# Moving the first token shift and the first weights' low parts to TensorE products with diagonal matrices

## The chip, the core and the metric

The program runs on one core of a Trainium2 chip. The metric is the device time of that core in microseconds. A core has TensorE (matmul, PE in the profile), VectorE (DVE), ScalarE (ACT), GpSimd (POOL) and SyncE (SP, which here only issues DMAs).

## The reference, cut to what matters

Three layers follow one another. Inputs are float32 but for the three weights of the second layer, which come as float64.

```python
# 1: attention in chunks of 64, B=8, H=8, S=576, D=64
scores = scale * q_c @ k_c.T ; attn = softmax(scores) ; x = attn @ v_c
# 2: token shift and channel mix, d_model 512, d_ff 1024
xk = mu_k * x + (1 - mu_k) * x_prev ; xr = mu_r * x + (1 - mu_r) * x_prev
k = relu(xk @ w_k) ; v = (k * k) @ w_v ; x = sigmoid(xr @ w_r) * v
# 3: causal attention of 4 experts, the best two of each token weighted by a gate
```

x_prev is x one token earlier in the same sequence, and zero for the first token.

## The kernel before

All products of layers 2 and 3 are made in three reduced-precision (float32r) products: every operand is kept as a high part `hi` (the value rounded to float32r) and a low part `lo = value - hi`, and `mm3` (L53) adds hi·hi, hi·lo and lo·hi.

Layers 1 and 2 are in `attn_mix` (L62). Tokens are cut into 36 tiles of 128 and 12 units of 384. Attention runs on pairs of tiles j: `s_T` (L132) transposes q and k of a tile on TensorE, `s_S` (L144) makes the scores of a pair and its softmax, with five VectorE steps and an exponential on ScalarE, `s_PT` (L138) transposes the probabilities, and `s_PV` (L173) multiplies by v and copies the result into `XT`, a unit's x with channels on partitions. `s_prev` (L211) puts the token before a unit into column 0 of `XT`. The list `attn` (L337) holds these steps in program order: pair 2 is transposed (tiles 4 and 5), then the probabilities of tiles 2 and 3 are turned, and one step `s_SPV` makes the scores of pair 2 and then the v products of pair 1, which complete unit 0.

`s_shift` (L222) makes the shifted input of a unit for w = 1 (xr) and w = 0 (xk), in four groups of 128 channels: ScalarE scales x_prev by 1 - mu, VectorE multiplies x by mu and adds (L240), ScalarE rounds the sum to `hi` (L243), VectorE subtracts for `lo` (L244). `mix_r`, `mix_k` and `mix_v` (L251, L259, L278) are the matmuls of a unit: 48, 96 and 96 products of 128 x 384. Their PSUM tiles are the three buffers with the tag "mix".

The float64 weights are brought to float32 in 20 conversions of 128 x 512 (four of w_r, eight of w_k, eight of w_v): `conv` (L296) loads the raw words over the SP queue into a staging tile `st`, which has two buffers after the first four, and works on ScalarE (L310), GpSimd (L311) and VectorE (L312 to L314); `split` (L322) rounds to `hi` on GpSimd (L46) and subtracts for `lo` on VectorE (L324).

The string `pro` orders the prologue: c is one conversion, a is one step of `attn`, q and v are loads, s is the shift of unit 0. After it, the items of each unit are issued in order, and attention steps are put between them at `rate0` a matmul item for the first two units, and conversions two an item in `mix_r` and one after. This program order is only a priority: the build orders every engine's stream on a simulated time line, and on the chip each engine then takes its stream in that order.

Layer 3 (`experts`, L449) begins behind the last unit and is not touched.

Of the kernel before, what the change touches and what calls it, by code (L numbers as in the profile page):

```python
# [8 lines left out]
F32 = mybir.dt.float32  # L9
F32R = mybir.dt.float32r  # L10
I32 = mybir.dt.int32
ACTF = mybir.ActivationFunctionType
ALU = mybir.AluOpType
# [6 lines left out]

CH = 64
UNIT = 384
CFG = dict(ps=(2, 3, 1, 2), P=5, sm=3, load=6, lag=(3, 4), out=(5, 1), qk1=(1, 1), qk0=(10, 1.2), v=(11, 1), order=(3, 4, 0, 1, 2), after=1, conv='v', clo='v', chi='g', x2hi='g', x2lo='v', ylo='g', yhi='v', xt='aa', r2='av', klo='vg', amul='vg', nearly=2, x2b=1, yb=4, qb=4, direct=((0, 1), (1, 1), (1, 1)), tailAV=4, kp=1, yt=1, yf=2, zb=1, om=(4, 3, 2, 1, 0), hp=1000, x2d=2, early=(2, 1), dact=3, rate0=0.43, rate=0.45, sh=(10, 12, 2), sh2=(11, 1, -1), pro='cccqqaacavvcaaaaacaacaaaascc', alag=2, seq=0, end=2, outL=(10, 2), outE=2, kcp='aa', dsc='v', ldb=2, vb=2, cn=512, stb=2, xb=4, pa=5, tb=2, first_j=7)
SEG = 192


# [7 lines left out]
def eng(nc, c):  # L34
    return nc.vector if c == "v" else nc.gpsimd


def nth(s, i):
    return s[i % len(s)]


def copy(nc, c, out, in_):
    if c == "a":
        nc.scalar.activation(out=out, in_=in_, func=ACTF.Copy)
    else:
        eng(nc, c).tensor_copy(out, in_)  # L46


def f32(ap):
    return ap.bitcast(F32)  # L50


def mm3(nc, out, terms, first=True, last=True):  # L53

    n = len(terms)
    for i, ((ah, al), (bh, bl)) in enumerate(terms):
        nc.tensor.matmul(out=out, lhsT=ah, rhs=bh, start=first and i == 0, stop=False)  # L57
        nc.tensor.matmul(out=out, lhsT=ah, rhs=bl, start=False, stop=False)  # L58
        nc.tensor.matmul(out=out, lhsT=al, rhs=bh, start=False, stop=last and i == n - 1)  # L59


def attn_mix(tc, at, x2T, q, k, v, mu_k, mu_r, w_k, w_v, w_r, ident, attended_all, mixed_k):  # L62

    nc = tc.nc
# [3 lines left out]
    KD = DM // 128  # L68
    FF = w_k.shape[1]
    KF = FF // 128  # L70
    NU = B * S // UNIT
    TPU = UNIT // 128
    NSEG = UNIT // SEG
    CPS = SEG // CH
    scale = 1.0 / float(D) ** 0.5

    with ExitStack() as ctx:
        wts = ctx.enter_context(tc.tile_pool(name="wts", bufs=1))
        mx = ctx.enter_context(tc.tile_pool(name="mx", bufs=1))
        ps = ctx.enter_context(tc.tile_pool(name="psM", bufs=1, space=PSUM))  # L80

        pa_open = ExitStack()
        pa = pa_open.enter_context(tc.tile_pool(name="psA", bufs=1, space=PSUM, side="right"))
        wkr_open = ExitStack()
        wkr = wkr_open.enter_context(tc.tile_pool(name="wkr", bufs=1, side="right"))
# [4 lines left out]
        mu = wkr.tile([128, 2, KD], F32, name="mu")  # L90
        mu1 = wkr.tile([128, 2, KD], F32, name="mu1")
# [3 lines left out]
        def runs(t):  # L95
            b, s = divmod(t * 128, S)
            return [(0, b, s, 128)] if s + 128 <= S else [(0, b, s, CH), (CH, b + 1, 0, CH)]

        def load_qk(t):
            for src, nm in ((q, "q"), (k, "k")):  # L100
                x = at.tile([128, H * D], F32, tag="ld" + nm, bufs=CFG["ldb"], name="ld" + nm)
                for p, b, s, n in runs(t):
                    nc.sync.dma_start(out=x[p:p + n].rearrange("p (h d) -> p h d", h=H),
                                      in_=src[b, :, s:s + n, :].rearrange("h p d -> p h d"))
                qkv[nm, t] = x

        def load_v(t):
            x = at.tile([128, 2, HP, D], F32, tag="ldv", bufs=CFG["vb"], name="ldv")
            for c in range(2):
                b, s = divmod(t * 128 + c * CH, S)  # L110
                for e in range(2):
                    r = e ^ c
                    nc.sync.dma_start(out=x[r * 64:(r + 1) * 64, c],
                                      in_=v[b, e::2, s:s + CH, :].rearrange("g p d -> p g d"))
            qkv["v", t] = x

        qT, kT, PP, PT, XT = {}, {}, {}, {}, {}
        nT = NU * TPU

        def bank(nm):  # L120
            return pa.tile([128, HP, 128], F32, tag="A", bufs=CFG["pa"], name=nm)

        def to_sbuf(src, nm):

            p = bank("Tps")
            for g in range(HP):
                nc.tensor.transpose(p[:, g], src[:, g * 128:(g + 1) * 128], ident)  # L127
            o = at.tile([128, HP, 128], F32, tag=nm, bufs=CFG["tb"], name=nm)
            nc.scalar.activation(out=o, in_=p, func=ACTF.Copy)
            return o  # L130

        def s_T(t):  # L132
            qT[t] = to_sbuf(qkv.pop(("q", t)), "qT")
            kT[t] = to_sbuf(qkv.pop(("k", t)), "kT")
            if t + CFG["ldb"] < nT:
                load_qk(t + CFG["ldb"])

# [67 lines left out]
        def s_SPV(j):  # L205
            if 2 * j < nT:
                s_S(j)
            if j:
                s_PV(j - 1)

        def s_prev(u):  # L211
# [6 lines left out]
                    nc.gpsimd.tensor_copy(x[:, :, sg, 0:1], src[:, :, SEG:SEG + 1])  # L218

        XS = {}  # L220

        def s_shift(u, ws, g):  # L222
            x = XT[u]
            now, prev = x[:, g, :, 1:], x[:, g, :, :SEG]
            by_act = u < CFG["dact"]
            if not by_act:
                d = wkr.tile([128, NSEG, SEG], F32, tag="xa", bufs=2, name="xa")
                nc.gpsimd.tensor_tensor(d, now, prev, op=ALU.subtract)  # L228
            for w in ws:
                nm = "kr"[w]  # L230
                if g == 0:
                    XS[u, w] = Split(wkr.tile([128, KD, UNIT], F32R, tag="xh" + nm, name="xh" + nm),
                                     wkr.tile([128, KD, UNIT], F32R, tag="xl" + nm, name="xl" + nm))
                o = XS[u, w]
                a = d if not by_act and w == ws[-1] else wkr.tile([128, NSEG, SEG], F32, tag="xa" if by_act else "r2", bufs=2, name="xb")
                af = a.rearrange("p s t -> p (s t)")
                m = mu[:, w, g:g + 1]
                if by_act:
                    nc.scalar.activation(out=a, in_=prev, func=ACTF.Copy, scale=mu1[:, w, g:g + 1])
                    nc.vector.scalar_tensor_tensor(a, now, m, a, op0=ALU.mult, op1=ALU.add)  # L240
                else:
                    nc.vector.scalar_tensor_tensor(a, d, m, prev, op0=ALU.mult, op1=ALU.add)  # L242
                nc.scalar.activation(out=o.hi[:, g], in_=af, func=ACTF.Copy)  # L243
                nc.vector.tensor_tensor(o.lo[:, g], af, f32(o.hi[:, g]), op=ALU.subtract)  # L244
# [3 lines left out]
        def rhs(o, g):  # L248
            return o.hi[:, g], o.lo[:, g]

        def mix_r(u, m):  # L251
# [3 lines left out]
            cc = slice(m * 128, (m + 1) * 128)  # L255
            mm3(nc, p, [((wr.hi[:, g, cc], wr.lo[:, g, cc]), rhs(XS[u, 1], g)) for g in range(KD)])
            nc.scalar.activation(out=sig[u][:, m], in_=p, func=ACTF.Sigmoid)  # L257

        def mix_k(u, m):  # L259
            p = ps.tile([128, UNIT], F32, tag="mix", bufs=3, name="mps")  # L260
            cc = slice(m * 128, (m + 1) * 128)
            mm3(nc, p, [((wk.hi[:, g, cc], wk.lo[:, g, cc]), rhs(XS[u, 0], g)) for g in range(KD)])
            r = mx.tile([128, UNIT], F32, tag="r", bufs=2, name="r")
# [30 lines left out]
        done = [0]  # L294
# [26 lines left out]

        def split(z, dst, g, c0, n):  # L322
            copy(nc, CFG["chi"], dst.hi[:, g, c0:c0 + n], z)
            eng(nc, nth(CFG["clo"], done[0])).tensor_tensor(dst.lo[:, g, c0:c0 + n], z, f32(dst.hi[:, g, c0:c0 + n]), op=ALU.subtract)  # L324

        def chunks(src, dst):
# [10 lines left out]
        attn = []  # L337
        for j in range(nT // 2 + 1):
            two = (2 * j, 2 * j + 1)
            attn += [(t // TPU, s_T, t) for t in two if t < nT]  # L340
            attn += [((t - 2) // TPU, s_PT, t - 2) for t in two if t > 1]
            attn.append(((2 * j - 1) // TPU if j else 0, s_SPV, j))
            attn += [(t // TPU, s_prev, t // TPU) for t in (2 * j - 2, 2 * j - 1) if t > 0 and t % TPU == TPU - 1]
        attn.reverse()

        def attend(u, n=1):
# [22 lines left out]
        loads = {"q": iter(range(CFG["ldb"])), "v": iter(range(CFG["vb"]))}  # L369

        def first_shift():
            for ws in ((1, 0),) if CFG["sh2"][2] >= 0 else ((1,), (0,)):
                for g in range(KD):
                    s_shift(0, ws, g)

        for c in CFG["pro"]:
            if c == "a":
                attend(2)
            elif c == "c":
                convert(1)  # L380
            elif c in loads:
                (load_qk if c == "q" else load_v)(next(loads[c]))
            else:
                attended(0)
                first_shift()

        credit = 0.0
        for u in range(NU):
# [6 lines left out]
            for i, (f, *args) in enumerate(items):  # L395
# [10 lines left out]
                if u + 1 < NU:  # L406
                    both = u + 1 <= CFG["sh2"][2]
                    for ws, at0 in (((1, 0), CFG["sh2"][0]),) if both else (((1,), CFG["sh"][0]), ((0,), CFG["sh"][1])):
                        g, r = divmod(i - at0, CFG["sh2" if both else "sh"][1 if both else 2])
# [478 lines left out]
```

## Time and profile before

| | |
|---|---|
| Median of 3 runs | 1052.54 us (1049.31 to 1054.02) |
| Profiled execution | 1051.87 us, span 1050.1 us |
| PE busy | 992.5 us of the span |
| DVE, ACT, POOL busy | 721.4, 583.4, 414.7 us |
| mean granted TensorE clock | 0.990 |

Busy time of TensorE is from the start of an instruction to its modelled end. It overlaps for pipelined instructions, so the pace is read from the distance of starts. Times in rows are microseconds from the start of the span unless they are marked ns.

### The profile page before, as it was taken

How to read it: one execution, taken by the hardware profiler on the slowest of the kernel's cores; microseconds unless marked ns; L12 is line 12 of the kernel's file. 1: busy time of each engine (PE TensorE's matmuls, PEld its weight loads, DVE VectorE, ACT ScalarE, POOL GpSimd, SP SyncE). 2: the span in 40 equal slices, each digit the busy share in tenths (PEclk: the TensorE clock that was granted, in tenths of full speed). 3: DMA queues.
4: the chain of work that ended last, by engine and by line, in shares of the span. 5: the costliest groups of instructions: out<-in, count | busy, mean ns of one | idle time of the engine just before them, and what ended most of it. 6: DMA issues, size and time to landing. Idle time of an engine off the chain costs nothing.

```text
span 1050.1 us, 22252 instructions
## 1 busy us (share of the span) xinstructions
PE 992.5 (95%) x8422; PEld 951.1 (91%) x8422; DVE 721.4 (69%) x1793; ACT 583.4 (56%) x1379; POOL 414.7 (39%) x507
## 2 busy tenths in 40 slices
PE   3679899999999999999999999999999999999997
PEld 2569899998999999999998999999999898998985
DVE  5899745628654856665667622787878687878896
ACT  3479473545354445545353422576776667766674
POOL 5444403526443744454545536423333332313201
PEclk9889999999999999999999999999999999999999
DMA  9774512242323243323213025645361635334212
GB/s 227 201 196 133 128 33 81 49 114 62 101 61 100 49 115 82 81 72 75 65 44 86 16 61 134 133 115 147 73 180 48 189 63 161 102 98 139 71 54 72
DMA packets 167522, 105.27 MB, mean 100 GB/s; under 512 B 133512, under 2 KB 145912, under 8 KB 167416
## 3 DMA queue, kind: packets, MB, share of 16 engines
q1 hardware_dynamic: 132024, 54.55, 20.3%
q0 software_dynamic: 35392, 49.30, 18.0%
q8 instruction: 67, 1.10, 0.4%
q14 instruction: 39, 0.32, 0.1%
HBM read 66.01 MB, written 28.38 MB: 90 GB/s over the span
## 4 chain that ended last, share of the span: by engine, by line
PE 64%; DVE 18%; DMA 6%; ACT 6%; issue 3%; POOL 2%; SPq 0%; ACTq 0%; DVEq 0%; POOLq 0%
PE mps L57 12%; PE mps L59 12%; PE mps L58 12%; PE pj L57 5%; PE pj L58 4%; PE pj L59 4%; PE Tps L663 3%; PE Tps L127 3%; PE AVps L687 2%; DMA out_dram<-o 2%; PE AVps L683 2%; DVE r L271 2%; DVE sm L605 2%; PE Sps L603 1%; PE Sps L602 1%
## 5 line engine op out<-in xcount | busy, mean ns | idle before, releaser
L57 PE MATMUL mps<-xhk,wkh 128*128 128x384 f32 x384 | 131.6, 343 | 0.2
L57 PE MATMUL mps<-kh,wvh 128*128 128x384 f32 x384 | 130.4, 343 | 1.2 <-DVE x2o L288 0.8
L58 PE MATMUL mps<-kl,wvh 128*128 128x384 f32 x384 | 128.9, 337 | 2.5 <-POOL kl L273 2.4
L58 PE MATMUL mps<-xlk,wkh 128*128 128x384 f32 x384 | 129.1, 337 | 0.0
L59 PE MATMUL mps<-xhk,wkl 128*128 128x384 f32 x384 | 128.8, 336 | 0.0
L59 PE MATMUL mps<-kh,wvl 128*128 128x384 f32 x384 | 127.5, 337 | 0.9 <-DVE wvl L324 0.9
L271 DVE TENSOR_TENSOR r<-r 128x384 f32<-128x384 f32 x80 | 65.8, 823 | 85.6 <-ACT r L264 85.6
L273 POOL TENSOR_TENSOR kl<-r,kh 128x384 fp32r<-128x384 f32 x80 | 87.6, 1099 | 82.7 <-ACT kh L272 81.6
L615 ACT ACTIVATE P<-sm,nm 128x128 f32<-128x128 f32 (+4 forms) x160 | 91.2, 571 | 38.3 <-DVE nm L605 21.6
L228 POOL TENSOR_TENSOR xa<-XT 128x384 f32<-128x384 f32 x72 | 71.0, 993 | 61.0 <-DVE xlr L244 35.0
L605 DVE CUSTOM_DVE_ANT_0 sm<-Sps,mask 128x192 f32<-128x192 f32 (+3 forms) x192 | 83.5, 438 | 14.7 <-PE Sps L603 12.8
L272 ACT ACTIVATE kh<-r 128x384 fp32r<-128x384 f32 x96 | 50.7, 528 | 59.4 <-DVE r L271 58.9
L663 PE MATMUL Tps<-ident,P 128*128 128x128 f32 x480 | 81.3, 275 | 1.7 <-DVE P L624 0.6
L524 POOL DMA_DIRECT2D K<-Kp x64 | 34.8, 561 | 113.1 <-ACT Kp L517 112.6
L242 DVE SCALAR_TENSOR_TENSOR xa<-xa,mu,XT 128x384 f32<-128x384 f32 x72 | 67.2, 948 | 15.4 <-POOL xa L228 15.4
L58 PEld LDWEIGHTS mps<-kl,wvh 128*128 128x128 f32 x384 | 72.7, 189 | 4.0 <-POOL kl L273 4.0
L57 PEld LDWEIGHTS mps<-kh,wvh 128*128 128x128 f32 x384 | 72.5, 189 | 2.7 <-DVE x2o L288 1.2
L57 PEld LDWEIGHTS mps<-xhk,wkh 128*128 128x128 f32 x384 | 72.3, 188 | 1.3 <-ACT r L264 1.0
L59 PEld LDWEIGHTS mps<-kh,wvl 128*128 128x128 f32 x384 | 72.2, 189 | 1.2 <-DVE wvl L324 1.2
L58 PEld LDWEIGHTS mps<-xlk,wkh 128*128 128x128 f32 x384 | 72.3, 188 | 0.1
L59 PEld LDWEIGHTS mps<-xhk,wkl 128*128 128x128 f32 x384 | 72.2, 188 | 0.0
L57 PE MATMUL mps<-xhr,wrh 128*128 128x384 f32 x192 | 66.2, 347 | 5.9 <-ACT sig L257 3.3
(202 smaller groups left out, 2908.0 us busy)
## 6 DMA issues: line engine op xcount, KB each, us to landing
x2T<-x2d POOLq DMA_DIRECT2D x48, 384.0 KB, 3.2
x<-x2T POOLq DMA_DIRECT2D x32, 576.0 KB, 6.3
ldv<-in_v_dram SPq DMA_DIRECT2D x144, 64.0 KB
K<-Kp POOLq DMA_DIRECT2D x64, 144.0 KB, 3.1
ldq<-in_q_dram SPq DMA_DIRECT2D x32, 256.0 KB
ldk<-in_k_dram SPq DMA_DIRECT2D x32, 256.0 KB
out_dram<-o SPq DMA_DIRECT2D x32, 256.0 KB
st<-in_moe_w_k_dram SPq DMA_DIRECT2D x8, 512.0 KB
```

Source lines behind the costliest of these rows:

```text
L57: nc.tensor.matmul(out=out, lhsT=ah, rhs=bh, start=first and i == 0, stop=False)
L58: nc.tensor.matmul(out=out, lhsT=ah, rhs=bl, start=False, stop=False)
L59: nc.tensor.matmul(out=out, lhsT=al, rhs=bh, start=False, stop=last and i == n - 1)
L228: nc.gpsimd.tensor_tensor(d, now, prev, op=ALU.subtract)
L242: nc.vector.scalar_tensor_tensor(a, d, m, prev, op0=ALU.mult, op1=ALU.add)
L271: eng(nc, CFG["r2"][u >= CFG["nearly"]]).tensor_tensor(r2, r, r, op=ALU.mult)
L272: nc.scalar.activation(out=o.hi, in_=r2, func=ACTF.Copy)
L273: eng(nc, CFG["klo"][u >= CFG["nearly"]]).tensor_tensor(o.lo, r2, f32(o.hi), op=ALU.subtract)
L524: nc.gpsimd.dma_start(out=d[half[j]], in_=t[half[i]])
L605: nc.vector.tensor_tensor_reduce(out=sm[:n, a:a + w], in0=pp[:n, :w], in1=mk[:, a:a + w], op0=ALU.add, op1=ALU.min, scale=-scale, scalar=3e38,
L615: nc.scalar.activation(out=x[:n, :nk], in_=sm[:n, :nk], func=ACTF.Exp, scale=-1.0, bias=nm[:n, :1], accum_out=z)
L663: nc.tensor.transpose(pp[:, j - j0], x[:, o:o + 128], ident)
```

## The change

Sixteen 128 x 128 diagonal matrices (mu and 1 - mu, for two inputs and four channel groups) and a negative identity are made once, in buffers that later hold `kh` and `kl`. Unit 0's shift becomes, for each input and group, two full float32 products of a diagonal with `XT` in PSUM; ScalarE rounds from there, and VectorE subtracts from there. For the first 12 conversions (w_r and w_k), `lo` becomes a float32 product of the identity with the value plus a float32r product of the negative identity with `hi`, in PSUM, copied out by ScalarE. In the list of attention steps, the turning and v products of pair 1 and the `s_prev` that follows now stand before tiles 4 and 5 are transposed and pair 2 is scored. `pro` has 7 conversions and 12 attention steps before the shift (before: 7 and 14, and 2 conversions behind it), and `rate0` goes from 0.43 to 0.5.

```diff
-rate0=0.43 ... pro='cccqqaacavvcaaaaacaacaaaascc'
+rate0=0.5 ... pro='cccqqaacavvcaaaaaccaaaas', pelo=12
         def s_SPV(j):
...
-            if j:
+            if j and j != 2:
                 s_PV(j - 1)
+        def diagonals():
+            x = [mx.tile([128, 3, 128], F32, tag=t, bufs=KF, name="dg") for t in ("kh", "kl") * 3]
+            DG.extend(y[:, i] for y in x[:-1] for i in range(3))
+            n = mx.tile([128, 128], F32R, tag="kh", bufs=KF, name="neg")
+            nc.vector.tensor_scalar(n, ident, -1.0, None, op0=ALU.mult)
+            DG.extend([x[-1][:, 0], n])
+            for w in (1, 0):
+                for g in range(KD):
+                    for i, y in enumerate((mu, mu1)):
+                        nc.scalar.activation(out=DG[(w * KD + g) * 2 + i], in_=ident, func=ACTF.Copy,
+                                             scale=y[:, w, g:g + 1])
+        def s_shift0(w, g):
...
+            p = ps.tile([128, UNIT], F32, tag="mix", bufs=3, name="xps")
+            ps3 = p.rearrange("p (s t) -> p s t", s=NSEG)
+            for i, a in enumerate((x[:, g, :, 1:], x[:, g, :, :SEG])):
+                nc.tensor.matmul(out=ps3, lhsT=DG[(w * KD + g) * 2 + i], rhs=a, start=i == 0, stop=i == 1)
+            nc.scalar.activation(out=o.hi[:, g], in_=p, func=ACTF.Copy)
+            nc.vector.tensor_tensor(o.lo[:, g], p, f32(o.hi[:, g]), op=ALU.subtract)
         def split(z, dst, g, c0, n):
             copy(nc, CFG["chi"], dst.hi[:, g, c0:c0 + n], z)
+            if done[0] <= CFG["pelo"]:
+                p = ps.tile([128, n], F32, tag="mix", bufs=3, name="cps")
+                nc.tensor.matmul(out=p, lhsT=ident, rhs=z, start=True, stop=False)
+                nc.tensor.matmul(out=p, lhsT=DG[-1], rhs=dst.hi[:, g, c0:c0 + n], start=False, stop=True)
+                nc.scalar.activation(out=dst.lo[:, g, c0:c0 + n], in_=p, func=ACTF.Copy)
+                return
...
+            if j == 2:
+                attn += turned + [(0, s_PV, 1)] + prevs
+                turned, prevs = [], []
+            attn += [(t // TPU, s_T, t) for t in two if t < nT] + turned
...
         def first_shift():
-            for ws in ((1, 0),) if CFG["sh2"][2] >= 0 else ((1,), (0,)):
+            for w in (1, 0):
                 for g in range(KD):
-                    s_shift(0, ws, g)
+                    s_shift0(w, g)
+        diagonals()
```

## Rows read from the trace of the kernel before

**Rows 1.** Windows: stretch, length, busy PE, PEld, DVE, ACT, POOL; clock; DMA share, GB/s
```profile
9.67:45.00 35.33, 20.24 (x250) 15.59 (x251) 28.18 (x45) 15.11 (x26) 16.56 (x17) 0.90 0.82 204
45.00:61.12 16.12, 11.50 (x288) 9.69 (x287) 14.29 (x23) 10.61 (x21) 7.13 (x7) 0.89 0.97 236
61.12:80.00 18.88, 14.93 (x168) 13.86 (x167) 17.63 (x31) 14.13 (x27) 6.41 (x5) 0.91 0.66 170
80.00:120.00 40.00, 37.14 (x378) 35.31 (x367) 38.69 (x65) 29.93 (x62) 17.16 (x15) 1.00 0.44 119
120.00:1042.00 922.00, 904.86 (x7352) 873.88 (x7344) 618.32 (x1626) 508.91 (x1238) 360.88 (x451) 1.00 0.35 90
```

**Rows 2.** PE timeline: start, length, instructions xcount, [idle before and what ended it]
```profile
9.67 1.09 PE L127 MATMUL Tps<-ident,ldq 128*128 128x128 f32 x4 [9.67 <-DMA ldq<-in_q_dram]
...
61.12 0.45 PE L57 MATMUL mps<-xhr,wrh 128*128 128x384 f32 x1
...
73.83 0.45 PE L57 MATMUL mps<-xhr,wrh 128*128 128x384 f32 x1 [3.33 <-ACT sig L257]
...
86.49 0.60 PE L127 MATMUL Tps<-ident,ldq 128*128 128x128 f32 x4
86.93 0.60 PE L127 MATMUL Tps<-ident,ldk 128*128 128x128 f32 x4
...
167.45 1.16 PE L154 MATMUL Sps<-kT,qT 64*64 64x64 f32 x64
168.43 0.68 PE L184 MATMUL PVps<-PT,ldv 64*64 64x64 f32 x32
...
170.12 0.33 PE L58 MATMUL mps<-xlr,wrh 128*128 128x384 f32 x1
170.29 0.34 PE L59 MATMUL mps<-xhr,wrl 128*128 128x384 f32 x1
```

**Rows 3.** PE groups by line in 0 to 45 us: xcount | busy, mean ns
```profile
L127 PE MATMUL Tps<-ident,ldk 128*128 128x128 f32 x24 | 6.8, 427 | 3.4 <-DMA ldk<-in_k_dram 3.3
L154 PE MATMUL Sps<-kT,qT 64*64 64x64 f32 x128 | 4.3, 316 | 1.0 <-ACT kT L129 1.0
L127 PE MATMUL Tps<-ident,P 128*128 128x128 f32 x10 | 2.3, 361 | 4.1 <-DVE P L168 4.1
L184 PE MATMUL PVps<-PT,ldv 64*64 64x64 f32 x64 | 1.9, 280 | 0.2 <-ACT PT L129 0.2
```

**Rows 4.** PE groups by line in 0 to 120 us
```profile
L127 PE MATMUL Tps<-ident,ldk 128*128 128x128 f32 x52 | 11.6, 347 | 3.7 <-DMA ldk<-in_k_dram 3.3 <-ACT qT L129 0.3
L154 PE MATMUL Sps<-kT,qT 64*64 64x64 f32 x384 | 11.4, 268 | 3.5 <-ACT kT L129 3.4
L58 PE MATMUL mps<-xlk,wkh 128*128 128x384 f32 x32 | 10.8, 343 | 0.0
L57 PE MATMUL mps<-kh,wvh 128*128 128x384 f32 x24 | 8.3, 347 | 0.0
L184 PE MATMUL PVps<-PT,ldv 64*64 64x64 f32 x320 | 8.1, 244 | 0.5 <-ACT PT L129 0.5
L127 PE MATMUL Tps<-ident,P 128*128 128x128 f32 x40 | 7.0, 298 | 6.1 <-DVE P L168 4.1 <-ACT XT L44 2.1
L58 PE MATMUL mps<-xlr,wrh 128*128 128x384 f32 x16 | 6.2, 385 | 0.6 <-DVE xlr L244 0.6
```

**Rows 5.** DVE groups by line in 0 to 120 us
```profile
L240 DVE SCALAR_TENSOR_TENSOR xb<-XT,mu,xb 128x384 f32<-128x384 f32 x16 | 9.9, 630 | 1.3 <-ACT xb L239 1.3
L324 DVE TENSOR_TENSOR wkl<-cz,wkh 128x512 fp32r<-128x512 f32 x8 | 6.2, 780 | 1.4 <-POOL wkh L46 1.4
```

**Rows 6.** ACT timeline: when unit 0's attention is copied into XT
```profile
54.06 1.19 ACT L44 ACTIVATE XT<-PVps 128x256 f32<-128x256 f32 x4
```

**Rows 7.** ACT groups by line in 0 to 45 us
```profile
L129 ACT ACTIVATE kT<-Tps 128x512 f32<-128x512 f32 x6 | 3.6, 598 | 1.3 <-PE Tps L127 1.3
```

**Rows 8.** Waits of SP's DMA queue in 0 to 80 us: total, times, longest
```profile
SPq L304 <- DVE cz L314: 19.0, 7, 6.6
```

More of the change, by code (lines that the diff above doesn't have):

```diff
@@ L22 @@
 UNIT = 384
-CFG = dict(ps=(2, 3, 1, 2), P=5, sm=3, load=6, lag=(3, 4), out=(5, 1), qk1=(1, 1), qk0=(10, 1.2), v=(11, 1), order=(3, 4, 0, 1, 2), after=1, conv='v', clo='v', chi='g', x2hi='g', x2lo='v', ylo='g', yhi='v', xt='aa', r2='av', klo='vg', amul='vg', nearly=2, x2b=1, yb=4, qb=4, direct=((0, 1), (1, 1), (1, 1)), tailAV=4, kp=1, yt=1, yf=2, zb=1, om=(4, 3, 2, 1, 0), hp=1000, x2d=2, early=(2, 1), dact=3, rate0=0.43, rate=0.45, sh=(10, 12, 2), sh2=(11, 1, -1), pro='cccqqaacavvcaaaaacaacaaaascc', alag=2, seq=0, end=2, outL=(10, 2), outE=2, kcp='aa', dsc='v', ldb=2, vb=2, cn=512, stb=2, xb=4, pa=5, tb=2, first_j=7)
+CFG = dict(ps=(2, 3, 1, 2), P=5, sm=3, load=6, lag=(3, 4), out=(5, 1), qk1=(1, 1), qk0=(10, 1.2), v=(11, 1), order=(3, 4, 0, 1, 2), after=1, conv='v', clo='v', chi='g', x2hi='g', x2lo='v', ylo='g', yhi='v', xt='aa', r2='av', klo='vg', amul='vg', nearly=2, x2b=1, yb=4, qb=4, direct=((0, 1), (1, 1), (1, 1)), tailAV=4, kp=1, yt=1, yf=2, zb=1, om=(4, 3, 2, 1, 0), hp=1000, x2d=2, early=(2, 1), dact=3, rate0=0.5, rate=0.45, sh=(10, 12, 2), sh2=(11, 1, -1), pro='cccqqaacavvcaaaaaccaaaas', pelo=12, alag=2, seq=0, end=2, outL=(10, 2), outE=2, kcp='aa', dsc='v', ldb=2, vb=2, cn=512, stb=2, xb=4, pa=5, tb=2, first_j=7)
 SEG = 192
@@ L220, in attn_mix @@
         XS = {}
+        DG = []
+        def diagonals():
[10 more added lines that the diff above has]
+        def s_shift0(w, g):
+            x = XT[0]
+            nm = "kr"[w]
+            if g == 0:
+                XS[0, w] = Split(wkr.tile([128, KD, UNIT], F32R, tag="xh" + nm, name="xh" + nm),
+                                 wkr.tile([128, KD, UNIT], F32R, tag="xl" + nm, name="xl" + nm))
+            o = XS[0, w]
+            p = ps.tile([128, UNIT], F32, tag="mix", bufs=3, name="xps")
[4 more added lines that the diff above has]
+            nc.vector.tensor_tensor(o.lo[:, g], p, f32(o.hi[:, g]), op=ALU.subtract)
         def s_shift(u, ws, g):
@@ L339, in attn_mix @@
             two = (2 * j, 2 * j + 1)
[L340 to L343, printed above, removed]
+            turned = [((t - 2) // TPU, s_PT, t - 2) for t in two if t > 1]
+            prevs = [(t // TPU, s_prev, t // TPU) for t in (2 * j - 2, 2 * j - 1) if t > 0 and t % TPU == TPU - 1]
+            if j == 2:
+                attn += turned + [(0, s_PV, 1)] + prevs
+                turned, prevs = [], []
+            attn += [(t // TPU, s_T, t) for t in two if t < nT] + turned
+            attn.append(((2 * j - 1) // TPU if j and j != 2 else 2 * j // TPU, s_SPV, j))
+            attn += prevs
         attn.reverse()
```

## The prediction

> **What bounds the kernel now.** I read the busy table by stretches first. From 120 us to 1042 us TensorE is busy 904.86 of 922 us, and no other engine is near that [rows 1]. So whatever the first 120 us save or lose moves the end by about as much, and what they hold is all that the change touches. In that stretch TensorE is not full: of 35.33 us from 9.67 to 45 it is busy 20.24, and even that flatters it.
>
> The timeline of TensorE shows why. It first runs at 9.67 us, when the first q has landed, and four transposes then take 1.09 us. Later, in a dense stretch, the next four start 0.44 us behind the first [rows 2]. That is more than a factor of two, while the granted clock of the stretch reads 0.90 [rows 1]. I go by the durations: before 45 us the engine mostly ran at 1.2 GHz, because it kept stopping.
>
> So I count work at the full pace, from distances of starts: 0.11 us a transpose, 0.98/64 = 0.0153 us an instruction of the 64 x 64 products, 0.173 us a float32r matmul of 384 columns [rows 2]. What is not work at that pace I call lost. Up to 45 us there are 48 transposes of q and k (the q row has the same 24 as the k row), 10 of probabilities and 192 small products [rows 3]: 5.3 + 1.1 + 2.9 = 9.3 us. Up to 120 us there are 104 and 40 transposes, 704 small products, and three passes of 32, 24 and 16 matmuls [rows 4]: 15.8 + 10.8 + 37.4 = 64.0 us. So the loss is 9.7 us before the first transposes, 35.3 - 9.3 = 26.0 us to 45 us, and 75 - 54.7 = 20.3 us from there to 120 us: 56.0 us. Of the 20.3, 11.4 are idle (4.6, 4.0 and 2.9 in the three stretches of rows 1), and 8.9 are slow pace and changes between kinds of work.
>
> What the engine waits for up to 61.12 us is the chain of unit 0. The copy into `XT` ends at 55.25 us [rows 6], the shift follows, and the first matmul of `mix_r` starts at 61.12 us [rows 2].
>
> **The change, part by part.** *Off VectorE.* Eight additions of L240 for unit 0 (8 x 0.63 = 5.0 us) and twelve subtractions of L324 (about 0.78 each, 9.4 us) go [rows 5]. VectorE is busy 28.2 of 35.3 us and 14.3 of 16.1 us in the stretches concerned [rows 1], so some of this lies on the chain of softmaxes. Nothing is paid there beyond one 128 x 128 negation, and L244 now reads PSUM; I take both at nothing because VectorE gains fourteen.
>
> *Onto ScalarE.* Sixteen diagonals, twelve copies of 512 columns from PSUM (a like copy takes 0.60 us [rows 7], 7.2 us in all), less eight scalings. ScalarE is busy 15.1 of 35.3 us up to 45 us [rows 1]. The diagonals wait for mu and ident and fall into the time before the first q and k, and the copies into its gaps. If that cover is gone they delay the copies of qT and kT that sit behind them in ScalarE's stream, at up to 0.6 us each; this is in the range, not in the sum.
>
> *Onto TensorE.* Sixteen float32 products of 384 columns, twelve float32 and twelve float32r products of 512. No row shows a full-size float32 product. From below it is one pass at the float32r pace, 0.173 us for 384 columns; then everything is 16 x 0.173 + 24 x 0.23 = 8.3 us. The small float32 products stand in the trace with two instructions for each one written (64 a pair of tiles, 32 in the code), and a float32 transpose, which is one instruction, needs 0.11 us for 128 columns. Two such passes are 0.66 us for 384 columns and 0.88 for 512. I take this, since it is the nearest row of the same type: 16 x 0.66 = 10.6, 12 x (0.88 + 0.23) = 13.3, together 23.9 us. From above it is twice that, 47.8 us, if all of it ran at 1.2 GHz.
>
> The Trainium skill (FP8 and Floating Point Precision, TensorE Precision Notes) says that true float32 takes four passes through the array. By that a product would take 0.69 us at 384 columns and the sum would be 24.9 us, one more than mine; no run here shows it. It speaks against the change, which buys VectorE time at four passes of the bounding engine.
>
> *Earlier unit 0.* The transposes of tiles 4 and 5 and the scores of pair 2 go behind the v products of pair 1 in priority. They are not saved, only moved into the dense part. Their loads are issued from `s_T` of tiles 2 and 3 as before, so SP's order there changes little. On SP it is the staging loads that wait: 19.0 us for VectorE's L314, because there are two staging buffers [rows 8]. That loop sets the pace of the conversions, and L324 is not in it; I give the conversions no gain.
>
> *When unit 0 is ready.* L240 comes too late to help `XT`. About four of the L324 lie between the softmaxes of pairs 0 and 1 (3 us), pair 2's softmax no longer competes, and ScalarE's copy into `XT`, which stood behind a conversion step, has one less in front of it. I estimate 55.25 - 9 = 46 us. From there TensorE has the 16 products, the last four conversions and `mix_r` in hand, all without another softmax.
>
> *The sum.* Equal time allows a loss of 56.0 - 23.9 = 32.1 us. The first 9.7 stay. Up to 45 us, eight conversions' products (8.9 us) go into time that was lost anyway, and the shorter chain brings some 3.7 us of attention work forward: 26.0 - 12.6 = 13.4 us. After 45 us the idle 11.4 is filled by 15 us of products but for 1.5 (the 3.3 us at 73.83, where `mix_r` waits for its first sigmoid [rows 2], falls behind them), and of 8.9 of slow pace the half stays, 4.5. Together 29.1 us, so 3.0 us less than allowed. The profiled execution took 1051.87 us (span 1050.1 and 1.8 around it), which becomes 1048.9; it lay 0.7 below the median, so the forecast is 1049.5 us.
>
> `rate0` costs nothing that I can see: attention runs some three steps further ahead in two units, and these steps must be done by the eleventh either way.
>
> **The rivals.** *The chain shortens more.* Then unit 0 is ready at 40 us and the products start at once. For it: VectorE loses 14 us of its 60 up to 61 us. Against it: k and v still come from DMA queues that are 0.82 to 0.97 busy [rows 1]. It gives another 6 us of lost time: 1043.5 us.
>
> *The clock rises earlier.* TensorE is stopped so often before 45 us that 20.2 us of busy time do 9.3 us of work. Eight conversions' products in these gaps may bring it to 2.4 GHz; a set of four transposes on the chain would then take 0.44 instead of 1.09 us, and with six sets on the chain 4 us more come off: 1045.5 us. The Trainium skill (TensorE: Matmul & The Clock Gate, Why this matters for your kernels) asks for dense work and no idle gaps to keep the fast clock. The trace agrees so far that the slow transposes stand where the engine idles.
>
> *Slower: the products stand in front.* The program issues all 16 products, of xr and of xk, ahead of `mix_r`, and TensorE takes its stream in order. Before, VectorE and ScalarE made the xk half while TensorE ran `mix_r`. If the 16 run at 1.2 GHz, another 10.6 us are lost, less the 3 gained: 1060 us. It decides where a product takes more than 0.66 + 3.0/16 = 0.85 us. For it speaks that the stretch from 55 us on was slow in places; against it, that the products themselves are dense.
>
> *Nothing.* The conversion loop [rows 8] delivers the last low parts of w_v when it did before, and TensorE waits there instead: 1052.5 us.
>
> **How the numbers follow.** My forecast 0.43, shorter chain 0.17, clock 0.13, products in front 0.15, nothing 0.12. A measurement of this kernel can tell about 0.5% from no change, 5.3 us, so faster is below 1047.2 and slower above 1057.8. Around the forecast lie 4 us to each side, for the ScalarE copies and the uncertain 46 us, so a quarter of its chance counts as faster: 0.11 + 0.17 + 0.12 makes 0.40. Slower takes the products in front and a little of the forecast: 0.18. The rest, 0.42, is same. The range must hold the shorter chain and the clock, and most of the way to the slower case: 1040 to 1058 us.
>
> **What would show it.** Right: the first `mix_r` matmul near 57 us with 16 products right before it, float32 instructions at about 0.33 us start to start, no wait of 3 us for the sigmoid, VectorE's busy time to 120 us down by some 12 us, and TensorE at 99% from 110 us on. Wrong: products at twice that distance, `XT` complete later than 50 us because a copy waits behind a `cps` copy on ScalarE, or a new wait of TensorE for w_v's low parts.

## Result, and the profile after

The changed kernel takes 1062.55 us (median of 5 runs, 1061.13 to 1066.02) against 1052.54 before. The ratio is 1.0112 [1.0083, 1.0141], so it is slower, by 10 us between the medians. The forecast was 1049.5 us in a range of 1040 to 1058: the sign and the range were both missed. The profiled execution took 1062.55 us with a span of 1060.6.

| | before | after |
|---|---|---|
| span | 1050.1 us | 1060.6 us |
| PE busy | 992.5 us | 1016.0 us |
| DVE, ACT, POOL busy | 721.4, 583.4, 414.7 us | 709.7, 596.8, 409.1 us |
| mean granted TensorE clock | 0.990 | 0.984 |

The windows of the kernel after, with the columns of [rows 1] and one stretch of 5 us added:

```profile
9.67:45.00 35.33, 25.37 (x295) 16.36 (x293) 23.82 (x38) 20.52 (x42) 17.36 (x18) 0.80 0.87 205
45.00:61.12 16.12, 15.81 (x154) 11.30 (x154) 9.13 (x16) 9.34 (x19) 0.81 (x2) 0.91 0.71 156
61.12:80.00 18.88, 17.05 (x192) 13.07 (x191) 11.96 (x22) 12.71 (x24) 7.36 (x7) 0.91 0.59 148
80.00:120.00 40.00, 38.41 (x334) 36.44 (x333) 36.31 (x57) 31.34 (x61) 19.38 (x18) 1.00 0.47 135
75.00:80.00 5.00, 5.00 (x20) 4.23 (x19) 3.05 (x6) 4.40 (x11) 3.49 (x4) 0.66 0.69 192
120.00:1042.00 922.00, 905.42 (x7451) 875.27 (x7450) 616.85 (x1613) 511.91 (x1238) 357.57 (x452) 1.00 0.35 91
```

From 120 to 1042 us TensorE is as busy as before: 905.42 us of 922, against 904.86 [rows 1]. VectorE is relieved as meant: its four stretches from 9.67 to 120 us add up to 81.2 us, before 98.8. TensorE is fuller than before in each of the four. It is busy with more work, and not with the old work sooner.

The groups of TensorE from 0 to 120 us (count, then busy time and mean ns, then idle time before them and its releaser) show the new work, which has no answer in [rows 4]:

```profile
L356 PE MATMUL cps<-cz,ident 128*128 128x512 f32 x24 | 16.4, 774 | 10.8 <-DVE cz L344 10.7
L248 PE MATMUL xps<-XT,dg 128*128 128x384 f32 x32 | 10.9, 489 | 0.0
L357 PE MATMUL cps<-wkh,neg 128*128 128x512 f32 x8 | 5.5, 683 | 1.5 <-POOL wkh L46 1.5
L357 PE MATMUL cps<-wrh,neg 128*128 128x512 f32 x4 | 2.4, 608 | 0.0
```

The timeline of TensorE after, to be laid beside [rows 2]:

```profile
14.31 0.60 PE L127 MATMUL Tps<-ident,ldq 128*128 128x128 f32 x4
...
23.38 1.09 PE L127 MATMUL Tps<-ident,ldq 128*128 128x128 f32 x4 [4.85 <-DMA ldq<-in_q_dram]
...
48.87 4.04 PE L248 MATMUL xps<-XT,dg 128*128 128x384 f32 x12
...
62.95 1.02 PE L356 MATMUL cps<-cz,ident 128*128 128x512 f32 x2
...
66.42 1.12 PE L356 MATMUL cps<-cz,ident 128*128 128x512 f32 x2
...
67.61 0.34 PE L57 MATMUL mps<-xhr,wrh 128*128 128x384 f32 x1
...
73.93 0.69 PE L184 MATMUL PVps<-PT,ldv 64*64 64x64 f32 x32 [1.77 <-ACT PT L129]
74.68 1.49 PE L356 MATMUL cps<-cz,ident 128*128 128x512 f32 x2
...
90.52 0.42 PE L57 MATMUL mps<-xhk,wkh 128*128 128x384 f32 x1
...
94.44 0.44 PE L57 MATMUL mps<-xhk,wkh 128*128 128x384 f32 x1 [1.59 <-ACT sig L287]
```

The products start at 48.87 us. The first `mix_r` comes 18.7 us later, at 67.61 us, where it was 61.12 before. `mix_k` starts at 90.52 us (before 77.57), `mix_v` at 109.55 (99.55), unit 1 at 132.08 (124.96). From there the delay hardly grows: 7.1 us at unit 1, 8.3 at unit 2 (177.67 against 169.34), 8.4 at unit 11 (620.51 against 612.09). The last 2.1 of the 10.5 us of span come behind the start of unit 11: from there to the end it is 440.1 us against 438.0. In two variants below, with the same work there, it took 435.8 us (e8) and 438.3 (e1), so that part can't be put down to the change.

ScalarE and VectorE show where the conversions stand. ScalarE's timeline (start, length, tile, idle before it):

```profile
41.62 0.68 ACT L340 ACTIVATE cz<-st 128x512 f32<-128x512 f32 x1 [1.79 <-DMA st<-in_moe_w_k_dram]
...
46.27 1.22 ACT L44 ACTIVATE XT<-PVps 128x256 f32<-128x256 f32 x4 [2.51 <-PE PVps L184]
...
64.06 0.68 ACT L340 ACTIVATE cz<-st 128x512 f32<-128x512 f32 x1 [0.42 <-DMA ldq<-in_q_dram]
...
71.60 1.28 ACT L287 ACT_TABLE_LOAD   x1
72.90 0.49 ACT L287 ACTIVATE sig<-mps 128x384 f32<-128x384 f32 x1
73.28 0.59 ACT L129 ACTIVATE PT<-Tps 128x512 f32<-128x512 f32 x1
...
89.61 0.61 ACT L358 ACTIVATE wkl<-cps 128x512 fp32r<-128x512 f32 x1
90.23 1.28 ACT L163 ACT_TABLE_LOAD   x1
91.53 1.06 ACT L163 ACTIVATE P<-P 128x1024 f32<-128x1024 f32 x1
92.60 1.28 ACT L287 ACT_TABLE_LOAD   x1
```

VectorE's timeline, the last step of two conversions (it writes z, the value that is then split):

```profile
41.68 0.69 DVE L344 SCALAR_TENSOR_TENSOR cz<-st,cz 128x512 int32<-128x512 int32 x1
...
45.46 0.69 DVE L344 SCALAR_TENSOR_TENSOR cz<-st,cz 128x512 int32<-128x512 int32 x1
```

`XT` is complete at 47.5 us (before 55.25, [rows 6]). But two finished values z, of 42.4 and 46.2 us, lie in both buffers of z until TensorE reads them at 62.95 and 66.42 us: their products stand behind all sixteen of the shift in its stream. ScalarE can begin the next conversion only when the first has been read (62.95 + 1.02 = 63.97; L340 starts at 64.06), so no conversion starts for 22 us. The row names a load as releaser; by the distance of 0.09 us it is more likely this buffer. The last low part of w_k lands at 89.61 + 0.61 us, where before the last one started at 67.96. The last 3.6 us of this are ScalarE's own: the product ends at 85.96 us, and its copy stands behind conversion steps that wait for loads of w_v.

`mix_k` starts just behind it, but does not wait for it. A conversion holds 512 of w_k's 1024 output channels, so the first four of the eight `mix_k` need only conversions 5 to 8; in e12 below `mix_k` starts before the last low part is written. TensorE's waits from 45 to 135 us (total, times, longest) name no part of w_k:

```profile
PE PVps L184 <- ACT PT L129: 1.8, 1, 1.8
PE mps L57 <- ACT sig L287: 1.6, 1, 1.6
PE Tps L127 <- DVE m L166: 0.2, 1, 0.2
```

Up to 90.52 us TensorE is busy with `mix_r`, products and attention steps that stand ahead of `mix_k` in its stream. Both longer waits end at ScalarE, right behind an ACT_TABLE_LOAD of 1.28 us. It stands in ScalarE's timeline where it goes from exponentials to sigmoids or back. Four of them lie between 45 us and unit 1, at 71.60, 90.23, 92.60 and 123.63 us, and before there were two.

The chain of waits of the kernel after goes through the conversions and the loads behind them, and enters TensorE at that sigmoid (start, length, what):

```profile
64.06 0.69 ACT cz L340
...
83.49 4.94 DMA st<-in_moe_w_v_dram
88.51 0.66 ACT cz L340
...
93.90 0.50 ACT sig L287
94.44 0.44 PE mps L57
```

### The profile page after: what moved, and what is told of

Same layout as the page of the kernel before. It is cut to its first block, busy times and chain, and to the rows that moved or that the text cites. A ratio compares the mean times of both kernels' runs of the same rounds, so it can differ in the third digit from the quotient of the medians.

```text
span 1060.6 us, 22373 instructions
## 1 busy us (share of the span) xinstructions
PE 1016.0 (96%) x8490; PEld 963.4 (91%) x8490; DVE 709.7 (67%) x1774; ACT 596.8 (56%) x1403; POOL 409.1 (39%) x507
## 3 DMA queue, kind: packets, MB, share of 16 engines
q1 hardware_dynamic: 132024, 54.55, 20.3%
## 4 chain that ended last, share of the span: by engine, by line
PE 70%; DVE 13%; DMA 7%; ACT 5%; issue 2%; POOL 2%; SPq 1%; ACTq 0%; DVEq 0%; POOLq 0%
PE mps L57 13%; PE mps L58 13%; PE mps L59 13%; PE pj L57 5%; PE pj L59 4%; PE pj L58 4%; PE Tps L127 3%; PE Tps L705 3%; PE AVps L729 2%; PE AVps L725 2%; DVE sm L647 2%; PE Sps L645 2%; PE Sps L644 2%; DMA out_dram<-o 1%; PE Sps L154 1%
## 5 line engine op out<-in xcount | busy, mean ns | idle before, releaser
L58 PE MATMUL mps<-xlk,wkh 128*128 128x384 f32 x384 | 129.0, 336 | 0.0
L59 PE MATMUL mps<-xhk,wkl 128*128 128x384 f32 x384 | 129.0, 336 | 0.0
L657 ACT ACTIVATE P<-sm,nm 128x128 f32<-128x128 f32 (+4 forms) x160 | 91.2, 571 | 37.8 <-DVE nm L647 20.6
L258 POOL TENSOR_TENSOR xa<-XT 128x384 f32<-128x384 f32 x72 | 67.5, 949 | 80.9 <-DVE xlr L274 52.9
L57 PE MATMUL mps<-xhr,wrh 128*128 128x384 f32 x192 | 67.6, 352 | 3.8 <-DVE x2o L318 3.8
```

The costliest lines, as they stand in the source:

```text
L657: nc.scalar.activation(out=x[:n, :nk], in_=sm[:n, :nk], func=ACTF.Exp, scale=-1.0, bias=nm[:n, :1], accum_out=z)
```

## Experiments

Theory H (hold; O in some expectations): the conversions are held in TensorE's stream, and `mix_k` waits for w_k. Rival P (price): the 23 us of added work on the bounding engine alone costs the 10 us. Each ratio is to the kernel before, run on the same chip, with its 95% interval. In the table, XT is when unit 0's input is complete, w_k when the last low part of w_k starts to be written, and the last column has the first matmuls of `mix_r`, of `mix_k`, of unit 1 and of unit 3, all in us. These four times are from the one traced execution of each kernel.

| run | median | ratio | XT | w_k | mix_r, mix_k, units 1 and 3 |
|---|---|---|---|---|---|
| before | 1052.54 | | 55.25 | 67.96 | 61.1, 77.6, 125.0, 218.5 |
| after | 1062.55 | 1.0112 [1.0083, 1.0141] | 47.5 | 89.61 | 67.6, 90.5, 132.1, 226.5 |
| e2_order_only | 1058.2 | 1.0064 [1.0045, 1.0083] | 55.7 | 62.02 | 58.8, 75.3, 123.5, 223.6 |
| e3_lo_only | 1052.89 | 1.0013 [0.9996, 1.0030] | 53.2 | 78.07 | 68.4, 84.1, 129.5, 222.8 |
| e4_shift_only | 1070.52 | 1.0187 [1.0161, 1.0213] | 62.5 | 65.53 | 85.3, 95.6, 137.7, 238.8 |
| e5_no_shift | 1054.66 | 1.0040 [1.0021, 1.0058] | 51.8 | 75.86 | 54.4, 76.7, 123.9, 223.3 |
| e6_no_lo | 1061.41 | 1.0087 [1.0057, 1.0117] | 57.4 | 61.65 | 73.4, 82.0, 126.7, 227.7 |
| e7_old_order | 1059.93 | 1.0089 [1.0064, 1.0113] | 49.4 | 94.50 | 75.8, 97.3, 139.5, 229.3 |
| e1_one_pass | 1066.1 | 1.0143 [1.0118, 1.0168] | 50.0 | 90.62 | 66.1, 91.2, 142.5, 236.6 |
| e8_pelo7 | 1052.74 | 1.0015 [0.9996, 1.0035] | 48.0 | 71.60 | 68.1, 79.0, 119.7, 221.5 |
| e10_pelo7_work | 1057.9 | 1.0064 [1.0040, 1.0088] | 48.6 | 71.71 | 69.7, 90.8, 130.2, 231.2 |
| e9_one_pelo7 | 1048.92 | 0.9977 [0.9961, 0.9993] | 52.2 | 70.44 | 62.0, 71.0, 117.8, 219.1 |
| e11_pelo7_rate43 | 1051.98 | 1.0010 [0.9990, 1.0031] | 49.3 | 72.48 | 67.2, 78.2, 123.5, 224.6 |
| e12_lo7_only | 1055.05 | 1.0032 [1.0012, 1.0052] | 56.4 | 76.52 | 64.3, 75.6, 133.2, 222.1 |
| e16_lo7_order | 1055.45 | 1.0054 [1.0033, 1.0075] | 55.5 | 69.36 | 59.0, 75.3, 129.0, 225.8 |
| e13_conv_first | 1073.84 | 1.0228 [1.0205, 1.0250] | 47.5 | 73.81 | 92.6, 104.8, 138.1, 238.2 |
| e14_one_conv_first | 1050.51 | 1.0003 [0.9986, 1.0019] | 49.6 | 66.51 | 75.1, 84.4, 122.1, 223.0 |
| e15_pelo7_xr_only | 1049.98 | 0.9999 [0.9985, 1.0013] | 48.6 | 70.85 | 56.8, 71.1, 122.0, 221.6 |

The start of unit 1 alone does not give the end: how much attention has been done by then differs between variants. By the start of unit 3 all have done the same (72 transposes each of q and k, 448 instructions of v products). A traced execution need not lie at its median: e8's took 1048.63 us, 4.1 below, and e10's 1062.37, 4.5 above. In nine of the sixteen runs (e4, e5, e6, e7, e9, e10, e12, e13, e15) the median lies in none of the ranges expected.

**One part alone.** e2 takes the new list, `pro` and `rate0` into the kernel before; e3 its low parts; e4 its shift:

```diff
 e2: -rate0=0.43, pro='cccqqaacavvcaaaaacaacaaaascc', old attn
     +rate0=0.5, pro='cccqqaacavvcaaaaaccaaaas', new attn
 e3: before, +if done[0] <= 12: ... cps products
 e4: after, -pelo=12 +pelo=0, old attn, pro and rate0
```

> The kernel before with the new order of attention steps, the new prologue string and rate0 = 0.5 alone; shift and low parts as before. Theory P: no work is added, unit 0 is ready earlier, 1048 to 1053 us. Rival O: the new order itself delays w_k's conversions behind the shift, so that mix_k starts late, 1056 us or above.

> The kernel before with the low parts of w_r and w_k as products alone. Theory P: 13.4 us of work come, eight conversions' share (9 us) falls into gaps before 45 us, so 1055 to 1058 us. Rival O: with the old order the conversions are early enough, 1050 to 1053 us.

> The kernel before with unit 0's shift as products with diagonals alone. Theory P: 10.7 us of work come in front of mix_r, where TensorE waited about 5 us for the shift and 3 for the sigmoid, so 1055 to 1060 us. Rival O: 1050 to 1053 us, since the conversions keep their place.

The shift alone costs 1.87%, the new order 0.64%, the low parts nothing that can be told. That adds up to 2.6%, but together they cost 1.12%: the parts don't add. Each edit also lets the build order every stream anew, which is a likely reason and was not tested. e2's time is in the range of its rival, but not by its path: w_k and `mix_k` come earlier than before, and what costs the 0.64% stays open. The new order alone does not bring `XT` forward, as this timeline of ScalarE in e2 shows:

```profile
51.78 0.66 ACT L310 ACTIVATE cz<-st 128x512 f32<-128x512 f32 x1 [4.29 <-DMA st<-in_moe_w_k_dram]
...
54.47 1.20 ACT L44 ACTIVATE XT<-PVps 128x256 f32<-128x256 f32 x4
```

In e4 `XT` comes 7 us later than before, and the products stand behind it. The waits of ScalarE in e4 (total, times, longest) give a candidate, a load of raw weights in ScalarE's stream ahead of attention's copies, 20.3 us of waiting up to 90 us where before it was 5.7. What puts the loads there was not settled.

```profile
ACT cz L340 <- DMA st<-in_moe_w_k_dram: 20.3, 6, 6.0
```

**One part undone.** e5 makes unit 0's shift as before, e6 all low parts on VectorE, e7 has the old list, `pro` and `rate0`:

```diff
 e5: -s_shift0(w, g)
     +s_shift(0, ws, g)        (no diagonals)
 e6: -pelo=12 +pelo=0
 e7: after, old attn, pro and rate0
```

> The changed kernel with unit 0's shift as before (ScalarE and VectorE); the new order and the low parts as products stay. By now the shift alone costs 18 us, the order alone 6, the low parts alone nothing. If the parts add up, this takes 1058 to 1060 us. If the low parts as products make up for the order (TensorE is kept at its fast clock and VectorE is freed for the softmaxes), 1049 to 1053 us.

> The changed kernel with all low parts of weights on VectorE; the new order and the shift as products stay. If the parts add up: 1052 + 6 + 18 = 1074 to 1078 us. If the low parts as products are what delays w_k (conversions wait for TensorE's stream), this is below the changed kernel, under 1058 us.

> The changed kernel with the old order of attention steps, old prologue string and rate0 = 0.43; shift and low parts as products. If the parts add up: 1068 to 1072 us. If the order in the changed kernel costs what it costs alone, 1056 to 1058 us.

Without the shift's products 0.7% of the 1.12% goes. Without the low parts' products, or with the old order, the loss is within the interval what it was. In e6 w_k is early (61.65) and `XT` late (57.4); in e7 it is the other way round (94.50 and 49.4). In these two an early unit 0 and early weights were not had together. For theory H e6 is a miss: no weight waits for TensorE there, and most of the loss stays.

**The price alone.** e1 keeps the program order, and reads only the upper 16 bits of both operands of the float32 products, as bf16, so one pass:

```diff
-lhsT=DG[(w * KD + g) * 2 + i], rhs=a
+lhsT=top(DG[(w * KD + g) * 2 + i]), rhs=top(a)
-lhsT=ident, rhs=z
+lhsT=top(ident), rhs=top(z)
```

> The changed kernel, but its float32 products (the sixteen of the shift, the twelve with the identity) read only the upper 16 bits of both operands as bfloat16, so that each is one pass; lower bits are left out. Theory P (the price of the products on the bounding engine): TensorE's work falls by 16 x (0.67 - 0.17) + 12 x (0.89 - 0.23) = 15.9 us and the time with it, to about 1047 us, faster than the kernel before. Rival O (their place in TensorE's stream, the shared PSUM buffers and the late conversions): the freed time turns into waits, at least half of it, and the time stays at 1055 us or above.

P alone expected 1047 us and fails here: the lower price did not give the time back. The groups of TensorE in e1 up to 120 us:

```profile
L361 PE MATMUL cps<-cz,ident 128*128 128x512 bf16 x12 | 5.9, 494 | 14.6 <-DVE cz L349 14.6
...
L253 PE MATMUL xps<-XT,dg 128*128 128x384 bf16 x16 | 3.8, 359 | 0.0
```

Instructions halve and busy time falls from 27.3 to 9.7 us, yet the kernel is not faster, and TensorE waits more. ScalarE's timeline in e1 shows w_k as late as after:

```profile
90.62 0.59 ACT L363 ACTIVATE wkl<-cps 128x512 fp32r<-128x512 f32 x1
```

But from 45 us to unit 1 TensorE is idle for 15.8 us, where after it was 3.7. Most of that is for other things, 6.9 us for `PT`, and only 1.8 for a part of w_k. The streams were ordered anew here too, so e1 does not show which wait hides the price.

**The held conversions.** e8 lets only seven conversions use products, so conversions 8 to 12 go to VectorE as before. e10 is e8 with products of the same columns, on constants, in the place of those five; nothing reads them. e9 is e8 with e1's edit (upper bits only). e11 is e8 with the old `rate0`:

```diff
 e8:  -pelo=12
      +pelo=7
 e10: e8, and
+            if CFG["pelo"] < done[0] <= 12:
+                p = ps.tile([128, 4, 128], F32, tag="mix", bufs=3, name="idle")
+                for i in range(4):
+                    nc.tensor.matmul(out=p[:, i], lhsT=ident, rhs=ident, start=True, stop=False)
+                    nc.tensor.matmul(out=p[:, i], lhsT=DG[-1], rhs=DG[-1], start=False, stop=True)
 e11: -rate0=0.5 +rate0=0.43
```

> The changed kernel with the low parts of the first seven conversions as products and of the other twelve-and-one on VectorE as before, so that no conversion behind the shift waits in TensorE's stream. If the held conversion buffers make w_k late (mix_k started at 90.5 us, before at 77.6): mix_k starts by 80 us and the time is at most 1054 us. If only the work counts, five products less are 5.6 us: 1057 us.

> Seven conversions' low parts as products, and for the other five of w_k products of the same number of columns on constants, whose output nobody reads: TensorE has the work of the changed kernel again, but no conversion buffer waits for it and ScalarE copies nothing out. If the held buffers cost the 10 us: 1052 to 1056 us. If the five products' work costs them: 1058 us or above.

> The kernel with seven conversions' low parts as products (the five behind the shift on VectorE again), and its float32 products in one pass on the upper 16 bits (lower bits are left out). TensorE's work falls by 16 x 0.5 + 7 x 0.66 = 12.6 us against that kernel, which took 1052.7. If price and late conversions limit together, so that each shows once the other is gone: 1040 to 1045 us. If the price is still hidden by waits: 1050 us or above.

> Seven conversions' low parts as products, with rate0 back at 0.43. If the pace of attention steps is of no weight: 1051 to 1054 us, as with 0.5. If 0.5 crowds the first units: 1048 to 1050 us.

e8 takes nearly all of the loss away, 1.0112 to 1.0015. VectorE's timeline in e8, and TensorE's, show the last low part of w_k 18 us earlier and `mix_k` 11.5 us earlier than after:

```profile
71.60 0.68 DVE L360 TENSOR_TENSOR wkl<-cz,wkh 128x512 fp32r<-128x512 f32 x1
```

```profile
79.00 0.34 PE L57 MATMUL mps<-xhk,wkh 128*128 128x384 f32 x1
```

That removes the hold and 5 x (0.86 + 0.23) = 5.5 us of work at once. e10 puts the work back without the hold, and ends between them, at 1.0064. So by the medians about half of the loss came with the five products' work, and half with what else e10 leaves out, the hold among it. The intervals leave 0.2 to 0.8% for the first and 0.1 to 0.9% for the second.

The traces do not show the second half. Unit 3 starts at 221.50 us in e8 and at 226.47 after. The 5.0 us between them are no more than the 5.5 us of the five products, as if these cost nearly their full price where they stand, and the hold nothing beside it. The rest of the difference between the two traces lies further on, where the work is the same. In e10, without the hold, unit 3 starts later still, at 231.21 us. TensorE's timeline in e10 shows why:

```profile
76.38 1.18 PE L184 MATMUL PVps<-PT,ldv 64*64 64x64 f32 x32 [2.76 <-ACT PT L129]
77.48 0.79 PE L363 MATMUL idle<-ident 128*128 128x128 f32 x2
...
90.82 0.34 PE L57 MATMUL mps<-xhk,wkh 128*128 128x384 f32 x1
```

```profile
75.00:80.00 5.00, 3.62 (x44) 3.50 (x45) 4.23 (x8) 3.47 (x6) 2.22 (x2) 0.62 0.21 70
```

The low part of w_k is there at 71.71 us as in e8, and yet `mix_k` starts at 90.82, as late as after: early weights alone do not make it early. The dummy products took 9.4 us instead of 5.5. 5.2 us of this came right behind a wait of 2.76 us, where the window shows a granted clock of 0.62, part at 1.2 and part at 2.4 GHz. In this execution work put into this place also paid for the slow clock behind a wait. e9 shows that in e8's place the price counts: with the products at a quarter of the price (six of e1's shift instructions in 1.20 us, about 0.17 each, where the float32 product took 0.65), 0.4% comes back, to 0.9977. `rate0` alone makes no difference (e11).

**The same without the shift's products.** e12 is e3 with seven instead of twelve, e16 is e5 with seven:

```diff
-pelo=12
+pelo=7
```

> The kernel before with the low parts of the first seven conversions as products, shift and order as before. All twelve took 1052.9 with this order. They fall into gaps of the first 45 us and relieve VectorE there; nothing behind the shift waits for them: 1047 to 1050 us if the freed VectorE time shows, 1051 to 1053 us if not.

> Seven conversions' low parts as products and the new order of attention, with the whole shift of unit 0 as before. Sixteen products less against the kernel that took 1052.7: 1046 to 1050 us if their work counts, 1053 to 1057 us if the shift on VectorE is late instead.

Here seven is no better than twelve (1.0032 against 1.0013, 1.0054 against 1.0040). So the products of conversions 8 to 12 showed a cost only together with the shift's sixteen.

**Place and price together.** e13 issues five conversions ahead of the shift instead of behind it; e14 adds e1's edit:

```diff
-pro='cccqqaacavvcaaaaaccaaaas'
+pro='cccqqaacavvcaaaaaccaaaacccccs'
```

> The changed kernel with the five last conversions of w_k ahead of the shift in program order (prologue string ...aaaacccccs), all twelve low parts as products as in the changed kernel. The products' work is unchanged, but no conversion buffer waits behind the sixteen products of the shift. If waiting behind them costs 5 of the 11 us: 1055 to 1058 us. If the five products' work alone counts, wherever it stands: 1061 to 1064 us.

> The same with the float32 products in one pass on the upper 16 bits (lower bits are left out). One pass alone left the changed kernel at 1066, one pass with the five conversions on VectorE took 1048.9. If the late conversions were the limit that hid the price: 1047 to 1053 us. If one pass does not help wherever the conversions stand: 1056 us or above.

TensorE's timeline in e13:

```profile
57.16 0.63 PE L127 MATMUL Tps<-ident,ldq 128*128 128x128 f32 x4 [1.94 <-DMA ldq<-in_q_dram]
...
62.26 1.13 PE L356 MATMUL cps<-cz,ident 128*128 128x512 f32 x2 [1.47 <-DVE cz L344]
...
66.16 1.30 PE L127 MATMUL Tps<-ident,P 128*128 128x128 f32 x5 [2.36 <-DVE P L168]
...
71.37 2.74 PE L248 MATMUL xps<-XT,dg 128*128 128x384 f32 x8
```

The weights are early, 73.81 us, and `XT` as early as after. But the shift's products now stand behind those of the conversions and the attention steps between them, with waits of 1.94 us for a load, 1.47 for a conversion and 2.36 for a softmax, and start at 71.37 us. In each order TensorE's stream delays one or the other. For each place, at the full price and at a quarter of it: behind the shift's products 1.0112 and 1.0143, ahead of them 1.0228 and 1.0003, on VectorE 1.0015 and 0.9977. The lower price brings time in the last two places and none in the first; what hides it there is not shown. From e13 to e14 the time falls by 23.3 us, more than the 16 us of work taken out, so the streams' order has a part in these differences too.

**Half the shift.** e15 is e8 with the xk half made as before on ScalarE and VectorE, while TensorE runs `mix_r`:

```diff
-s_shift0(w, g)
+s_shift0(w, g) if w else s_shift(0, (0,), g)
```

> Seven conversions' low parts as products and only the xr half of the shift as products; the xk half on ScalarE and VectorE as before, beside mix_r. Eight products less are 5.4 us of work in the dense stretch: 1046 to 1049 us if the work there counts in full, 1051 to 1054 us if the xk half is late instead.

`mix_r` starts at 56.8 us, the 57 of the forecast, and `mix_k` at 71.1. The time is 0.9999 [0.9985, 1.0013]: even this gains nothing over the kernel before. No variant that computes everything in full beat it.

## Why the prediction was wrong

*What bounds the kernel.* Right: 7.1 of the 10.5 us of span are there by unit 1, and TensorE is as full behind it as before. Counted by the same paces to the start of unit 1, before has 68.8 us of work and 56.2 lost, after 92.0 and 40.1. So 23.2 us of work came and 16.1 of loss went: 7.1 us later, which the starts show. The forecast was that 26.9 us of loss would go (56.0 to 29.1).

*The slow clock before 45 us.* The comparison of 1.09 with 0.44 us sets a length against a distance of starts. Length to length it is 1.09 to 0.60 us, and distance to distance 0.88 (25.41 to 26.29 us) to 0.44. The factor is 1.8 to 2, so 1.2 GHz stands, but the rival that builds on it is worth 6 x 0.44 = 2.6 us and not 4.

*Onto TensorE.* Right in price. Twelve instructions of the shift's products take 4.04 us, (4.04 - 0.49)/11 = 0.323 us each, two to a product: 0.65 us where I took 0.66. The low parts took 24 x 0.43 + 12 x 0.23 = 13.1 us, together 23.4 against 23.9. Against the 0.173 us of a float32r matmul that is a factor of 3.7. The Trainium skill (FP8 and Floating Point Precision, TensorE Precision Notes) gives four passes for true float32; the trace agrees.

*Off VectorE, and when unit 0 is ready.* Right: 17.6 us less on VectorE, and `XT` at 47.5 us for a forecast of 46. But e2 shows that the new place of pair 2's softmax does not do it alone; with the new order and nothing else `XT` ends at 55.7.

*Up to 45 us.* Wrong: 19.0 us lost where I had 13.4, of which 10.0 idle and 9.0 slow pace (before 15.1 and 10.9). The 3.7 us of attention that the shorter chain was to bring forward did not come (9.4 us of it by 45 us, before 9.3), and seven conversions were done there, not eight.

*After 45 us.* Wrong, and the larger of the two failures by a little: 12.1 us lost up to unit 1, not 6.0. Of these 3.7 are idle, where I had 1.5, and 8.4 are slow pace and changes between kinds of work, where I had 4.5. The products filled the idle time, as meant, but the slow pace did not halve. The stretch to 61 us is full. The idle sits between 61 and 120 us, in waits of 1.77 us for `PT` and 1.59 for the sigmoid, both behind table loads of ScalarE, which no term of the sum counted. Part of the slow pace sits behind the first (granted clock 0.66 from 75 to 80 us; a pair of products took 1.49 us instead of 1.02).

*The steps that failed* are thus two terms of the sum, both on lost time: 13.4 us up to 45 us, which measured 19.0, and 1.5 + 4.5 us after it, which measured 3.7 + 8.4. The work was priced right, but only 16.1 us of it fell into time that was lost anyway. e8 shows where: the five products behind the shift stand in a stretch that was already full, and without them nearly all of the loss goes. e10 puts their work back, and half of the loss.

One sentence of *Earlier unit 0* failed as well: that L324 is not in the conversion loop, so that loop neither gains nor loses. Before, that was nearly so. After, z is read by TensorE, and its buffer comes free when TensorE's stream gets there. I had counted what TensorE must do for the low parts, and not what must wait for TensorE. The 22 us without a new conversion show this. That it costs time is not shown: in the changed kernel TensorE never waits for w_k up to 135 us, and e6 has no hold and most of the loss.

*The rivals.* "Products in front" gave 1060 us and came nearest, but not by its mechanism: it needed 0.85 us a product, and they took 0.65. What it had right is that all sixteen stand ahead of `mix_r`, and of the conversions too, which it did not say. Of 18.7 us between the first product and `mix_r` the sixteen take 10.3, two conversions 2.2, attention steps most of the rest. "Nothing" looked at the conversion loop and had it at its old pace. "The clock rises earlier" happened in part and was worth nothing: three sets of transposes up to 45 us took 0.60 us (at 14.31, 14.98 and 28.75), where before none did, but at 23.38 us, behind 4.85 us of waiting, one took 1.09 again, and no attention was done sooner. "The chain shortens more" set its 14 us against 60 us of VectorE up to 61 us; the rows give 60 up to 80 us and 42.5 from 9.67 to 61. The sum of the chances takes 0.12 for the clock's 0.13. None of the three signs of being wrong came; of the signs of being right the first failed: `mix_r` started at 67.6 us, not near 57.

What stays open: what the other half of the loss between e8 and after is, and whether the hold has a part in it; why the shift alone (e4) costs 18 us, more than with the rest of the change; why the order alone (e2) costs 6; and the 2 us behind unit 11.

## What to carry to other kernels

When a step moves to an in-order engine, its input buffers move with it: ask what stands ahead of the reader in that stream, and who needs the buffer back. Then look whether the bounding engine waits for what comes late: here it did not. Work on the bounding engine is free only while it waits anyway, and only if the place of the new work in its stream falls there; a price cut showed nothing in one place and 23 us in another, so test price and place together. Parts of a change measured alone did not add up here, where the build orders every stream anew.

## What the runs showed of the hardware

A full float32 product shows as two instructions in the trace, 0.323 us apart at 384 columns and 0.43 us at 512, and TensorE's float32 transposes of 128 columns as one of 0.11 us. Read as bf16 it is one instruction.

ScalarE's ACT_TABLE_LOAD took 1.28 us each time. After, both of TensorE's longer waits behind 45 us (1.77 and 1.59 us) ended right behind one.

After TensorE's waits of 1.77 us (after) and 2.76 us (e10), the stretch of 75 to 80 us showed granted clocks of 0.66 and 0.62, and products in it took 1.5 times or more their usual time. Such short waits I had counted at their own length. The Trainium skill (TensorE: Matmul & The Clock Gate, Why this matters for your kernels) warns of idle gaps between bursts of matmuls. The trace agrees and goes further, since these gaps are shorter than the one that the page names; in e10 earlier waits in the same stretch may have had a part.
